# Inner sums of w_out operands made in the last unit of the first product, and turned attention tensors in another layout

## The chip, the cores and the metric

The kernel runs on one core of a Trainium2 chip. The metric is the device time of one execution in microseconds (us); lower is better. TensorE (PE) multiplies matrices, VectorE (DVE), ScalarE (ACT) and GpSimd (POOL) work elementwise, and SyncE (SP) issues the DMAs.

## What is computed

Eight batches of attention with pooled keys and values feed one two-layer product with a "snake" activation. All tensors are fp32.

```python
# q, k, v: (B=8, H=8, S=576, D=64); k and v are averaged over groups of 8 rows: Sp = 72
scores = scale * q @ k_p.T
attn = softmax(scores)                    # 576 x 72 for each head
x = (attn @ v_p) laid out as (4608, 512)
h = x @ w_in                              # (512, 2048)
s = sin(alpha * h)
g = h + s * s / (alpha + 1e-9)
out = g @ w_out                           # (2048, 512)
```

## The kernel before

**Stages.** The 4608 tokens are cut into nine units of 512. The first product (x @ w_in, `hidden`) runs unit by unit, u = 0 to 8, and stores g in DRAM (`g_bridge`). Then the second product (g @ w_out, `outputs`) runs over the same nine units. Both use Strassen's scheme in Winograd's form: seven products of half-size blocks instead of eight. The second product uses it on two levels: each of its seven outer products has seven inner ones, and their right-hand operands are sums of blocks of w_out.

**The first product.** A unit has 28 slots: four groups J of seven products. One slot is four matmuls (line 484), which the trace shows as eight. The order of all engines in this stage is written out by hand. `carry(u)` gives a table of extra work by slot: during unit u the attention of batch u + 1 is computed between the products. Slots 1 to 6 hold the scores, slots 8 to 12 the softmax, slots 12 to 14 `turn` (DVE transposes of 32 x 32 blocks into the tile `tr`, line 276). In slots 14 and 15 `move` issues twelve DMAs that carry `tr` to `aT`, the transposed attention weights (line 285). In slots 21 to 24 `turn_q` transposes the q of batch u + 2 into the same tile `tr` (line 145) and moves it with sixteen DMAs (line 152). In slot 24 `values` multiplies `aT` with the pooled v (line 309). This path with DVE transposes holds for batches 2 to 7, that is for units 1 to 6.

After its product a slot leaves work for the next slot: sums of PSUM banks (lines 463 and 544, DVE), the sine and the squares (ACT). Five PSUM banks go round, and a product that needs a bank again waits until DVE or ACT has emptied it.

**w_out.** `load_w_out` is a generator. Its first step issues the four loads in unit 7. Its next four steps each scale a quarter of w_out (line 408) and make outer sums of it (line 410); its last two make the inner sums of operands 1 and 2 (`inner_w`, line 427). `run` advances it in slots 13 and 20 of unit 7 and slots 6, 13, 17 and 20 of unit 8. The inner sums of the other five operands are made in `outputs`, while its first unit runs (`if u == 0 and n < 5: self.inner_w(...)`).

**The second product.** Only the PE order is written by hand; a planner orders the others, DVE among them. The outer products come as `ORDER = (1, 2, 4, 6, 7, 5, 3)`, and their first steps are woven into the last slots of unit 8. For one outer product p, seven calls of `product` (line 747) accumulate into one bank and one tile `ps_y`, of which there are three. `outer` makes the left-hand sums from the four quarters of g (tiles `r`, `home`, `x`), `inner` the inner ones (tiles `xe`, `home`), `combine` puts the results together (tiles `c`, `o`). All their DVE instructions have line 707, the helper `tt`. The DMA of an output block has line 763.

Of the kernel before, what the change touches and what calls it, by code (L numbers as in the profile page):

```python
# [40 lines left out]
class Kernel:  # L41
# [86 lines left out]
    def turn_q(self, b, part):  # L128


        nc = self.nc
        qm = self.qm[b]
        main, rest = self.q_views(qm)
        if part == 0:
            self.tr = self.new_tr()
        tr = self.tr.rearrange("p (c hp t i) -> p c hp t i", hp=self.NP, t=5, i=32)[:, 0:4]
        if part < 2:
            for e in range(2):
                if part == 0:
                    out = tr[:, 2 * e:2 * e + 2, :, 0:4, :].rearrange("p k hp t i -> p hp t k i")  # L140
                    x = main[:, e::2].rearrange("p hp t (k i) -> p hp t k i", i=32)
                else:
                    out = tr[:64, 2 * e:2 * e + 2, :, 4, :].rearrange("p k hp i -> p hp k i")
                    x = rest[:, e::2].rearrange("p hp (k i) -> p hp k i", i=32)
                nc.vector.transpose(out=out, in_=x)
            return
        self.qt[b] = qt = self.qt_view(qm)
        for a in ((0, 1), (2, 3))[part - 2]:
            w = 160 if a < 2 else 128
            for c in range(4):  # L150
                flat = lambda x: x.rearrange("p hp t i -> p hp (t i)")[:, :, 0:w]
                nc.sync.dma_start(out=flat(qt[32 * c:32 * c + 32, a]), in_=flat(tr[32 * a:32 * a + 32, c]))

    def new_tr(self):
        return self.ap.tile([P, 24 * 5 * 32], F32, name="tr")[:]

    def qt_view(self, t):
        return t[:].rearrange("p (a hp t i) -> p a hp t i", hp=self.NP, a=4, t=5)

    def qt_tiles(self, b):  # L160

        return self.qt[b].rearrange("p a hp t i -> p (a hp t i)").rearrange("p (i hp n) -> p i hp n", i=5, hp=self.NP)

    def attention(self, b):
# [16 lines left out]
        def q_t(i):  # L181

            n = rows[i]
            pairs = self.qm[b][:n, i * H * D:(i + 1) * H * D].rearrange("p (hp d) -> p hp d", hp=NP)
            if b not in self.qt:
                self.qt[b] = self.qt_view(self.qp.tile([P, 5 * H * D], F32, name="q"))
            ps = self.ps_a.tile([P, NP, P], F32, name="ps_qt", tag="a")
            for hp in range(NP):
                nc.tensor.transpose(ps[:, hp, :n], pairs[:, hp], self.ident[:n, :n])  # L189
            nc.scalar.copy(out=self.qt_tiles(b)[:, i, :, :n], in_=ps[:, :, :n])  # L190

        def columns(hp, i):

            if b < 2:
                return [(c, self.qt_tiles(b)[:, i, hp, c:c + 64]) for c in range(0, rows[i], 64)]
            if i < 4:
                return [(64 * c, self.qt[b][:, i, hp, 2 * c:2 * c + 2].rearrange("p t i -> p (t i)")) for c in range(2)]
            return [(32 * a, self.qt[b][:, a, hp, 4]) for a in range(2)]

# [60 lines left out]
        def new_a():  # L260
            aT.append(self.ap.tile([Sp, 4, H, 5, 32], F32, name="aT"))

        def a_t(i, g):
            n = rows[i]
            ps = self.ps_a.tile([Sp, 4, P], F32, name="ps_at", tag="a")
            for hh in range(4):
                nc.tensor.transpose(ps[:, hh, :n], ex[:n, i, 4 * g + hh, 0:Sp], self.ident[:n, :n])  # L267
            cp = nc.scalar.copy if g == 0 else nc.vector.tensor_copy
            cp(out=aT[0][:, 0:n // 32, 4 * g:4 * g + 4, i, :].rearrange("k a h i -> k h a i"),
               in_=ps[:, :, :n].rearrange("k h (a i) -> k h a i", i=32))  # L270

        def turn(i):
            n = rows[i]
            if i == 0:
                self.tr = self.new_tr().rearrange("p (c h t i) -> p c h t i", c=3, h=H, i=32)
            nc.vector.transpose(out=self.tr[:n, :, :, i, :].rearrange("p c h i -> p h c i"),
                                in_=ex[:n, i].rearrange("p h (c i) -> p h c i", i=32))

        def move(part):
            for a in (2 * part, 2 * part + 1):  # L280
                w = 160 if a < 2 else 128
                for c in range(3):
                    m = min(32, Sp - 32 * c)
                    flat = lambda x: x.rearrange("k h t i -> k h (t i)")[:, :, 0:w]
                    nc.sync.dma_start(out=flat(aT[0][32 * c:32 * c + m, a]), in_=flat(self.tr[32 * a:32 * a + m, c]))  # L285

# [16 lines left out]
        def values(hp):  # L303
            vp = self.vp[b]
            ps = self.ps_a.tile([P, 4 * P], F32, name="ps_o", tag="a")
            for e in range(2):
                h = 2 * hp + e
                x = aT[0][:, :, h, 0:4, :].rearrange("k a t i -> k t a i" if b < 2 else "k t a i -> k t (a i)")
                nc.tensor.matmul(ps[64 * e:64 * e + 64, :], vp[:, h, :], x, start=True, stop=True)  # L309
            to_x(ps[:].rearrange("p (t j) -> p j t", t=4), hp, 0, 512)  # L310

        def values_rest():
            vp = self.vp.pop(b)
            ps = self.ps_a.tile([P, NP, 64], F32, name="ps_or", tag="a")
            for hp in range(NP):
                for e in range(2):
                    h = 2 * hp + e
                    nc.tensor.matmul(ps[64 * e:64 * e + 64, hp, :], vp[:, h, :], aT[0][:, 0:2, h, 4, :], start=True, stop=True)
            to_x(ps[:], slice(0, NP), 512, 64)
# [5 lines left out]
    def load_alpha(self, row, rows):  # L325
# [4 lines left out]
        self.rat = self.const.tile([P, self.K2], F32, name="rat")  # L330
        self.alb = self.new_tr()[:, 0:self.FF]
        self.al_row, self.al_rows = row[0:1], rows[:self.K2]
# [17 lines left out]
    def load_w_in(self):  # L350

        nc, h = self.nc, self.FF // 2
        blk = lambda n: self.wp.tile([P, 2, h], F32, name=n)
        a11, a12, a21, a22, s1, s2, s4 = (blk(n) for n in ("a11", "a12", "a21", "a22", "as1", "as2", "as4"))
        self.A = {1: a11, 2: a12, 3: s4, 4: a22, 5: s1, 6: s2, 7: a21}
# [37 lines left out]
    def load_w_out(self, wp):  # L393
# [22 lines left out]
        self.W = {}  # L416
        for p in (1, 2):
            yield
            self.inner_w(p, wp)
        yield  # L420

    def inner_w(self, p, wp):
        nc, NJ = self.nc, self.NJ
        x = self.wb[p]
        e = wp.tile([P, 3, NJ, P], F32, name=f"we{p}")
        b = lambda i, j: x[:, :, i - 1, j - 1, :]
        tt = lambda o, x, y: nc.vector.tensor_tensor(out=o, in0=x, in1=y, op=OP.subtract)
        t1, t2, t4 = (e[:, i] for i in range(3))
        tt(t1, b(1, 2), b(1, 1))
# [182 lines left out]
    def carry(self, u):  # L612
# [43 lines left out]
        elif u < last:  # L656
# [9 lines left out]
            for hp in range(4):  # L666
                at((0, 1, 3, 4)[hp], self.load_kv, "v", b, hp)
                if b < last:
                    at((12, 13, 14, 17)[hp], self.load_kv, "k", b + 1, hp)
                at(24, A.values, hp)  # L670
            at(24, A.values_rest)
            if b < last:
# [29 lines left out]
    def outputs(self):  # L702
# [41 lines left out]
        def product(st, q, out, start):  # L744
            A, W = st["A"][q], self.W[st["p"]][q]
            for J in range(self.NJ):
                nc.tensor.matmul(out, A[:, J, :], W[:, J, :], start=(start and J == 0), stop=(J == self.NJ - 1), skip_group_check=True)  # L747

# [3 lines left out]
        def combine(st):  # L752
# [22 lines left out]
            elif p in (2, 3):  # L775
                o = block("o", 4)
                add(o[:], c[1 if p == 2 else 3][:], x4)
                with_z(o)
                out(0, 0 if p == 2 else 1, o)
# [16 lines left out]
        for k in range(len(seq) + 1):  # L796
# [19 lines left out]
            if last:  # L816
                product(last, 5, last["yz"][:, 1, :], False)
                product(last, 4, last["x"][:, 2, :], False)
            if st:
                product(st, 6, x[:, 1, :], False)  # L820
# [3 lines left out]
                if k + 1 < len(seq) and seq[k + 1] not in A:  # L824
                    A[seq[k + 1]] = inner(seq[k + 1][0], ORDER[seq[k + 1][1]])
                if u == 0 and n < 5:
                    self.inner_w(ORDER[n + 2], self.gs)
# [11 lines left out]
    def run(self):  # L839
        nc, tc = self.nc, self.tc  # L840
        pool = lambda s, n, b, **kw: s.enter_context(tc.tile_pool(name=n, bufs=b, **kw))
        with ExitStack() as top:
# [7 lines left out]
            nc.gpsimd.memset(self.ones[:], 1.0)  # L850
            engines = {nc.tensor.engine, nc.vector.engine, nc.scalar.engine, nc.gpsimd.engine, nc.sync.engine}
            with ExitStack() as one:
                self.wp = pool(one, "wp", 1)
# [23 lines left out]
                for u in range(self.NU):  # L877
                    x = self.carry(u)
                    if u == self.B - 1:
# [5 lines left out]
                        next(w)  # L885
                        for i in (13, 20):
                            x[i].append(lambda: next(w))
                    elif u > self.B - 1:
                        for i in (6, 13, 17, 20):
                            x[i].append(lambda: next(w))  # L890
# [47 lines left out]
```

## Time and profile before

| what | value |
|---|---|
| median of 3 runs | 961.09 us (961.07 to 962.59) |
| profiled execution, own time | 961.07 us |
| its span | 959.3 us |
| PE busy | 937.3 us, 98% of the span |
| DVE busy | 675.1 us, 70% |
| ACT busy | 414.5 us, 43% |
| second product, from its first product to the end | 550.3 to 959.3 us |
| one unit of the first product (units 1 to 5), from one `values` to the next | 57.2 us |

The span runs from the first instruction to the last; 1.8 us of the execution's own time lie outside it. The granted TensorE clock is 1.000 over the whole span. "Busy" counts modelled ends of matmuls, which overlap, so a wait of PE is best read from the starts of two matmuls and from the idle time that the trace puts before one.

### The profile page before, as it was taken

Reading aid. Unit: us, or ns where it says so; the run is one execution under the profiler, and the core shown is the slowest. Engines: PE = TensorE matmul, PEld = TensorE weight load, DVE = VectorE, ACT = ScalarE, POOL = GpSimd, SP = SyncE. Lnnn points to the kernel's source line nnn. Section 1 sums busy time; section 2 is a strip of 40 time slices with the busy share of each in tenths; the row PEclk is TensorE's granted clock in tenths of the full one; section 3 lists DMA queues with packets and bytes.
Section 4 is the critical chain, followed back from the end, with each engine's and each line's share of the span. In section 5 each row is a group of like instructions: output and inputs, shape, how many; then the busy total and the mean of one; then the engine's idle time right before and its main releaser. Section 6 shows DMA issues by size and latency. Waiting matters only on the chain.

```text
span 959.3 us, 18142 instructions
## 1 busy us (share of the span) xinstructions
PE 937.3 (98%) x7259; PEld 833.8 (87%) x7259; DVE 675.1 (70%) x1070; ACT 414.5 (43%) x919; POOL 200.6 (21%) x215
## 2 busy tenths in 40 slices
PE   7999999999999999999999999999999999999998
PEld 4677787887878888787888888999999999999998
DVE  4889584766838576583366889968678685958684
ACT  4377466575756647576565531111111111111111
POOL 1718374443725445260000000000000000000000
PEclk9999999999999999999999999999999999999999
DMA  9537466766576664636615135324242434243200
GB/s 223 170 97 208 128 191 145 212 147 201 162 196 202 149 187 114 187 124 183 224 77 206 80 126 193 120 102 154 79 155 69 151 97 153 98 149 122 100 34 35
DMA packets 84038, 137.88 MB, mean 144 GB/s; under 512 B 10177, under 2 KB 49873, under 8 KB 79345
## 3 DMA queue, kind: packets, MB, share of 16 engines
q1 hardware_dynamic: 83920, 136.70, 46.8%
q8 instruction: 58, 0.95, 0.4%
q14 instruction: 26, 0.21, 0.1%
q10 hardware_dynamic: 34, 0.02, 0.0%
HBM read 74.47 MB, written 47.19 MB: 127 GB/s over the span
## 4 chain that ended last, share of the span: by engine, by line
PE 86%; DVE 6%; DMA 2%; POOL 2%; issue 1%; SPq 1%; ACT 1%; DVEq 0%; POOLq 0%
PE bank L484 39%; PE bank L747 28%; PE ps_y L747 11%; PE ps_o L309 3%; PE ps_sc L208 2%; POOL kvin L105 1%; DMA q<-in_q_dram 1%; SPq L285 1%; DMA kvin<-in_v_dram 1%; DVE sm L257 1%; DVE as L368 1%; DVE h L544 1%; DVE h L463 1%; PE ps_qt L189 1%; PE ps_at L267 1%
## 5 line engine op out<-in xcount | busy, mean ns | idle before, releaser
L484 PE MATMUL bank<-home,a 128*128 128x256 f32 x1152 | 266.3, 382 | 1.4 <-ACT bank L514 1.4
L484 PEld LDWEIGHTS bank<-home,a 128*128 128x128 f32 x1152 | 215.3, 190 | 35.1 <-ACT bank L514 2.1
L484 PE MATMUL bank<-home,as 128*128 128x256 f32 x864 | 201.6, 382 | 3.4 <-DVE as L368 1.6
L484 PEld LDWEIGHTS bank<-home,as 128*128 128x128 f32 x864 | 161.7, 190 | 27.3 <-ACT bank L502 2.9
L105 POOL TENSOR_TENSOR kvin<-kvin 72x512 f32<-72x512 f32 x112 | 130.1, 1162 | 179.1 <-DMA kvin<-in_v_dram 111.1
L463 DVE TENSOR_TENSOR h<-bank,p 128x512 f32<-128x512 f32 x72 | 49.1, 682 | 82.9 <-ACT s L492 54.2
L490 ACT ACTIVATE s<-h,rat 128x256 f32<-128x256 f32 x144 | 65.2, 500 | 88.8 <-DVE h L463 88.8
L747 PE MATMUL bank<-wb,home 128*128 128x128 f32 x712 | 92.1, 275 | 0.0
L747 PEld LDWEIGHTS bank<-wb,home 128*128 128x128 f32 x712 | 85.7, 192 | 0.0
L821 ACT COPY bank<-bank 128x128 f32<-128x128 f32 x63 | 15.8, 250 | 149.7 <-PE bank L747 149.7
L492 ACT ACTIVATE s<-s 128x512 f32<-128x512 f32 (+1 forms) x106 | 77.8, 768 | 1.1
L490 ACT ACTIVATE s<-bank,rat 128x256 f32<-128x256 f32 x144 | 60.1, 468 | 36.3 <-PE bank L484 25.7
L747 PE MATMUL bank<-wb,xe 128*128 128x128 f32 x512 | 67.6, 275 | 0.0
L747 PEld LDWEIGHTS bank<-wb,xe 128*128 128x128 f32 x512 | 62.4, 192 | 0.1
L747 PE MATMUL bank<-we,home 128*128 128x128 f32 x464 | 59.4, 276 | 1.1 <-DVE home L707 1.1
L834 ACT COPY bank<-bank 128x128 f32<-128x128 f32 x63 | 15.8, 250 | 96.6 <-PE bank L747 96.6
L747 PEld LDWEIGHTS bank<-we,home 128*128 128x128 f32 x464 | 55.6, 192 | 1.3 <-issue 1.3
L250 POOL TENSOR_TENSOR ex<-ex,sm 128x576 f32<-128x576 f32 (+1 forms) x38 | 42.5, 1149 | 44.7 <-ACT ex L239 25.5
L544 DVE TENSOR_TENSOR h<-h,s 128x1024 f32<-128x1024 f32 x36 | 44.8, 1244 | 0.0
L544 DVE TENSOR_TENSOR h<-bank,s 128x512 f32<-128x512 f32 x36 | 24.5, 681 | 25.3 <-ACT s L492 24.0
L813 ACT COPY bank<-ps_y 128x256 f32<-128x256 f32 x63 | 22.5, 357 | 39.0 <-PE ps_y L747 39.0
L514 ACT COPY bank<-bank 128x512 f32<-128x512 f32 x36 | 20.6, 572 | 39.4 <-PE bank L484 39.4
(139 smaller groups left out, 1434.2 us busy)
## 6 DMA issues: line engine op xcount, KB each, us to landing
g_bridge<-h SPq DMA_DIRECT2D x36, 1024.0 KB
r<-g_bridge SPq DMA_DIRECT2D x18, 1024.0 KB
home<-g_bridge SPq DMA_DIRECT2D x18, 1024.0 KB
out_dram<-o SPq DMA_DIRECT2D x36, 256.0 KB
q<-in_q_dram SPq DMA_DIRECT2D x8, 1024.0 KB
kvin<-in_k_dram SPq DMA_DIRECT2D x28, 288.0 KB
kvin<-in_v_dram SPq DMA_DIRECT2D x28, 288.0 KB
a<-in_moe_w_in_dram SPq DMA_DIRECT2D x16, 256.0 KB
```

Of the source, the lines that this page charges most:

```text
L105: (eng or nc.gpsimd).tensor_tensor(out=o, in0=t[:, :, 0:w], in1=t[:, :, w:2 * w], op=OP.add)
L208: nc.tensor.matmul(ps[e][r:r + q.shape[-1], hp, :], q[s], kb[s, hp, :], start=True, stop=True)
L250: eng.tensor_tensor(out=E(n, i, 0, H), in0=E(n, i, 0, H), in1=sm[:n].unsqueeze(2).to_broadcast([n, H, Sp]), op=OP.mult)
L309: nc.tensor.matmul(ps[64 * e:64 * e + 64, :], vp[:, h, :], x, start=True, stop=True)
L463: add = lambda o, x, y: nc.vector.tensor_tensor(out=o, in0=x, in1=y, op=OP.add)
L484: nc.tensor.matmul(ps[:, jj, :], self.A[p][:, kk, f * P:(f + 1) * P], x[:, kk, :], start=(start and jj == 0 and kk == 0), stop=(kk == 1), ...
L490: nc.scalar.activation(out=G.s[:, i, j, jj, :], in_=src[:, jj, :], func=AF.Sin, scale=self.rat[:, f:f + 1])
L492: square = lambda G, x: nc.scalar.activation(out=x, in_=x, func=AF.Square)
L514: nc.scalar.copy(out=G.b7[:], in_=G.b6[:])
L544: add = lambda o, x, y: nc.vector.tensor_tensor(out=o, in0=x, in1=y, op=OP.add)
L747: nc.tensor.matmul(out, A[:, J, :], W[:, J, :], start=(start and J == 0), stop=(J == self.NJ - 1), skip_group_check=True)
L813: nc.scalar.copy(out=x[:, 0:2, :], in_=yz[:, 0:1, :].to_broadcast([P, 2, P]))
```

## The change

There are four parts.

1. **Inner sums.** `load_w_out` makes five operands' inner sums, 1, 2, 4, 6 and 7, and does it in slots 10, 13, 14, 17 and 20 of unit 8. The sums of 4, 6, 7 and 5 go into slices of the w_in operands a11, a12 and s4 of which `hidden` has made its last use; these three tiles move to a pool that lasts to the end. Three quarters of w_out are scaled in unit 7 (slots 9, 14, 20), the fourth in slot 6 of unit 8. `outputs` makes the sums of operands 5 and 3 only; on DVE they end up before the outer sums of the second product's first unit.
2. **Layout.** In `tr`, the turned q and `aT` the head becomes the outer index and the row block the inner one. A transpose of q takes one instruction for all heads instead of two. The moves of 160 columns per head, which read and wrote 5120 contiguous bytes per partition for `aT` and 2560 for q, become runs of 640 bytes; the moves of 128 columns stay at 512 bytes.
3. **values.** In units 1 to 6 the four calls of `values` go from slot 24 to slots 23, 24, 24 and 25, and `values_rest` goes to slot 25. A call in a slot's table comes ahead of the slot's product.
4. **The last addition.** For outer product 3 the term z from `ps_y` is added to `c3` before the last sum instead of to the output after it.

```diff
@@ load_w_out
-        for p in (1, 2):
+        for p in (1, 2, 4, 6, 7):
             yield
             self.inner_w(p, wp)
@@ inner_w
-        e = wp.tile([P, 3, NJ, P], F32, name=f"we{p}")
-        t1, t2, t4 = (e[:, i] for i in range(3))
+        if p in (4, 6, 7, 5):
+            J = (4, 6, 7, 5).index(p)
+            t1, t2, t4 = (self.A[i][:, :, J * JW * P:(J + 1) * JW * P].rearrange("p k (j d) -> p k j d", j=2) for i in (1, 2, 3))
+        else:
+            e = wp.tile([P, 3, 2, 2, P], F32, name=f"we{p}")
+            t1, t2, t4 = (e[:, i] for i in range(3))
@@ turn_q
-                nc.vector.transpose(out=out, in_=x)
+            nc.vector.transpose(out=tr[:, 0:16, 0:4, :].rearrange("p (h k) t i -> p h t k i", k=2),
+                                in_=main.rearrange("p h t (k i) -> p h t k i", i=32))
...
-                nc.sync.dma_start(out=flat(qt[32 * c:32 * c + 32, a]), in_=flat(tr[32 * a:32 * a + 32, c]))
+                src = tr[32 * a:32 * a + 32, 0:16].rearrange("p (hp c) t i -> p hp c (t i)", c=4)[:, :, c, 0:w]
+                nc.sync.dma_start(out=qt[32 * c:32 * c + 32, :, a].rearrange("p hp t i -> p hp (t i)")[:, :, 0:w], in_=src)
@@ attention
-            aT.append(self.ap.tile([Sp, 4, H, 5, 32], F32, name="aT"))
+            aT.append(self.ap.tile([Sp, H, 4, 5, 32], F32, name="aT"))
...
-                    nc.sync.dma_start(out=flat(aT[0][32 * c:32 * c + m, a]), in_=flat(self.tr[32 * a:32 * a + m, c]))
+                    src = self.tr[32 * a:32 * a + m].rearrange("p (h c) t i -> p h c (t i)", c=3)[:, :, c, 0:w]
+                    nc.sync.dma_start(out=aT[0][32 * c:32 * c + m, :, a].rearrange("k h t i -> k h (t i)")[:, :, 0:w], in_=src)
@@ carry
-                at(24, A.values, hp)
-            at(24, A.values_rest)
+                at((23, 24, 24, 25)[hp], A.values, hp)
+            at(25, A.values_rest)
@@ combine and the loop of outputs
                 add(o[:], c[1 if p == 2 else 3][:], x4)
-                with_z(o)
+                if p == 2:
+                    with_z(o)
...
+                if last["p"] == 3:
+                    t, z = C[last["u"]][3], last["yz"]
+                    tt(t[:, :, 1, :], t[:, :, 1, :], z[:, 1:2, :].to_broadcast([P, 2, P]), OP.add)
...
-                if u == 0 and n < 5:
+                if u == 0 and n in (3, 4):
                     self.inner_w(ORDER[n + 2], self.gs)
@@ run
-                        for i in (13, 20):
+                        for i in (9, 14, 20):
...
-                        for i in (6, 13, 17, 20):
+                        for i in (6, 10, 13, 14, 17, 20):
```

More of the change, by code (lines that the diff above doesn't have):

```diff
@@ L134, in turn_q @@
         if part == 0:
[L135 to L145, printed above, removed]
+            self.tr = self.ap.tile([P, 24, 5, 32], F32, name="tr")
+        tr = self.tr
+        if part == 0:
+            nc.vector.transpose(out=tr[:, 0:16, 0:4, :].rearrange("p (h k) t i -> p h t k i", k=2),
+                                in_=main.rearrange("p h t (k i) -> p h t k i", i=32))
+            return
+        if part == 1:
+            nc.vector.transpose(out=tr[:64, 0:16, 4, :], in_=rest.rearrange("p h (k i) -> p (h k) i", i=32))
             return
@@ L150, in turn_q @@
             for c in range(4):
-                flat = lambda x: x.rearrange("p hp t i -> p hp (t i)")[:, :, 0:w]
-                nc.sync.dma_start(out=flat(qt[32 * c:32 * c + 32, a]), in_=flat(tr[32 * a:32 * a + 32, c]))
-    def new_tr(self):
-        return self.ap.tile([P, 24 * 5 * 32], F32, name="tr")[:]
+                src = tr[32 * a:32 * a + 32, 0:16].rearrange("p (hp c) t i -> p hp c (t i)", c=4)[:, :, c, 0:w]
+                nc.sync.dma_start(out=qt[32 * c:32 * c + 32, :, a].rearrange("p hp t i -> p hp (t i)")[:, :, 0:w], in_=src)
     def qt_view(self, t):
-        return t[:].rearrange("p (a hp t i) -> p a hp t i", hp=self.NP, a=4, t=5)
-    def qt_tiles(self, b):
-        return self.qt[b].rearrange("p a hp t i -> p (a hp t i)").rearrange("p (i hp n) -> p i hp n", i=5, hp=self.NP)
+        return t[:].rearrange("p (hp a t i) -> p hp a t i", hp=self.NP, a=4, t=5)
     def attention(self, b):
@@ L189, in q_t @@
                 nc.tensor.transpose(ps[:, hp, :n], pairs[:, hp], self.ident[:n, :n])
-            nc.scalar.copy(out=self.qt_tiles(b)[:, i, :, :n], in_=ps[:, :, :n])
+            nc.scalar.copy(out=self.qt[b].rearrange("p hp a t i -> p hp (a t i)")[:, :, P * i:P * i + n], in_=ps[:, :, :n])
         def columns(hp, i):
[L194 to L198, printed above, removed]
+            qt = self.qt[b].rearrange("p hp a t i -> p hp (a t i)")
+            if b < 2 or i < 4:
+                return [(c, qt[:, hp, (P if b < 2 else 160) * i + c:][:, :64]) for c in range(0, rows[i], 64)]
+            return [(32 * a, qt[:, hp, 160 * a + P:160 * a + 160]) for a in range(2)]
         def products(i):
@@ L268, in a_t @@
             cp = nc.scalar.copy if g == 0 else nc.vector.tensor_copy
-            cp(out=aT[0][:, 0:n // 32, 4 * g:4 * g + 4, i, :].rearrange("k a h i -> k h a i"),
-               in_=ps[:, :, :n].rearrange("k h (a i) -> k h a i", i=32))
+            cp(out=aT[0][:, 4 * g:4 * g + 4, 0:n // 32, i, :], in_=ps[:, :, :n].rearrange("k h (a i) -> k h a i", i=32))
         def turn(i):
@@ L274, in turn @@
             if i == 0:
-                self.tr = self.new_tr().rearrange("p (c h t i) -> p c h t i", c=3, h=H, i=32)
-            nc.vector.transpose(out=self.tr[:n, :, :, i, :].rearrange("p c h i -> p h c i"),
-                                in_=ex[:n, i].rearrange("p h (c i) -> p h c i", i=32))
+                self.tr = self.ap.tile([P, 24, 5, 32], F32, name="tr")
+            nc.vector.transpose(out=self.tr[:n, :, i, :], in_=ex[:n, i].rearrange("p h (k i) -> p (h k) i", i=32))
         def move(part):
@@ L283, in move @@
                     m = min(32, Sp - 32 * c)
-                    flat = lambda x: x.rearrange("k h t i -> k h (t i)")[:, :, 0:w]
-                    nc.sync.dma_start(out=flat(aT[0][32 * c:32 * c + m, a]), in_=flat(self.tr[32 * a:32 * a + m, c]))
+                    src = self.tr[32 * a:32 * a + m].rearrange("p (h c) t i -> p h c (t i)", c=3)[:, :, c, 0:w]
+                    nc.sync.dma_start(out=aT[0][32 * c:32 * c + m, :, a].rearrange("k h t i -> k h (t i)")[:, :, 0:w], in_=src)
         def to_x(ps, hp, t0, m):
@@ L307, in values @@
                 h = 2 * hp + e
-                x = aT[0][:, :, h, 0:4, :].rearrange("k a t i -> k t a i" if b < 2 else "k t a i -> k t (a i)")
+                x = aT[0][:, h, :, 0:4, :].rearrange("k a t i -> k t a i" if b < 2 else "k t a i -> k t a i")
                 nc.tensor.matmul(ps[64 * e:64 * e + 64, :], vp[:, h, :], x, start=True, stop=True)
@@ L317, in values_rest @@
                     h = 2 * hp + e
-                    nc.tensor.matmul(ps[64 * e:64 * e + 64, hp, :], vp[:, h, :], aT[0][:, 0:2, h, 4, :], start=True, stop=True)
+                    nc.tensor.matmul(ps[64 * e:64 * e + 64, hp, :], vp[:, h, :], aT[0][:, h, 0:2, 4, :], start=True, stop=True)
             to_x(ps[:], slice(0, NP), 512, 64)
@@ L330, in load_alpha @@
         self.rat = self.const.tile([P, self.K2], F32, name="rat")
-        self.alb = self.new_tr()[:, 0:self.FF]
+        self.alb = self.ap.tile([P, 24, 5, 32], F32, name="tr")[:].rearrange("p k t i -> p (k t i)")[:, 0:self.FF]
         self.al_row, self.al_rows = row[0:1], rows[:self.K2]
@@ L352, in load_w_in @@
         nc, h = self.nc, self.FF // 2
-        blk = lambda n: self.wp.tile([P, 2, h], F32, name=n)
+        blk = lambda n: (self.wq if n in ("a11", "a12", "as4") else self.wp).tile([P, 2, h], F32, name=n)
         a11, a12, a21, a22, s1, s2, s4 = (blk(n) for n in ("a11", "a12", "a21", "a22", "as1", "as2", "as4"))
@@ L422, in inner_w @@
     def inner_w(self, p, wp):
-        nc, NJ = self.nc, self.NJ
+        nc = self.nc
         x = self.wb[p]
-        e = wp.tile([P, 3, NJ, P], F32, name=f"we{p}")
-        b = lambda i, j: x[:, :, i - 1, j - 1, :]
+        b = lambda i, j: x[:, :, i - 1, j - 1, :].rearrange("p (k j) d -> p k j d", k=2)
         tt = lambda o, x, y: nc.vector.tensor_tensor(out=o, in0=x, in1=y, op=OP.subtract)
-        t1, t2, t4 = (e[:, i] for i in range(3))
+        if p in (4, 6, 7, 5):
[4 more added lines that the diff above has]
+            t1, t2, t4 = (e[:, i] for i in range(3))
         tt(t1, b(1, 2), b(1, 1))
@@ L746, in product @@
             for J in range(self.NJ):
-                nc.tensor.matmul(out, A[:, J, :], W[:, J, :], start=(start and J == 0), stop=(J == self.NJ - 1), skip_group_check=True)
+                nc.tensor.matmul(out, A[:, J, :], W[:, J // 2, J % 2, :], start=(start and J == 0), stop=(J == self.NJ - 1), skip_group_check=True)
         def block(n, bufs=1):
@@ L851, in run @@
             engines = {nc.tensor.engine, nc.vector.engine, nc.scalar.engine, nc.gpsimd.engine, nc.sync.engine}
+            self.wq = pool(top, "wq", 1)
             with ExitStack() as one:
```

## The prediction

> **What bounds the kernel now.** I read the busy shares first, then the waits of PE, then the chain that ended last and the timeline where the chain leaves PE.
>
> ```profile
> PE 937.3 (98%) x7259; PEld 833.8 (87%) x7259; DVE 675.1 (70%) x1070; ACT 414.5 (43%) x919; POOL 200.6 (21%) x215
> ```
>
> PE bounds the kernel. A gain must take a wait out of PE, and any new wait of PE adds its whole length. The waits of PE sum to 17 us, and most lie before 100 us, in code that the change hardly touches. Later there is one cluster, in the chain from 560 to 600 us (start, length, what):
>
> ```profile
> 566.03 2.20 DVE x L707
> ...
> 569.17 2.20 DVE x L707
> ...
> 571.43 2.06 issue
> 573.49 1.90 DVE home L707 x3
> 575.39 0.14 issue
> 575.53 3.82 PE bank L747 x32
> 579.35 2.27 issue
> 581.62 2.02 PE ps_y L747 x16
> ```
>
> Here the second product takes over. The "issue" pieces hide a cause, which the timeline of the same stretch names:
>
> ```profile
> 578.90 2.29 DVE L707 TENSOR_TENSOR home<-r,x 128x2048 f32<-128x2048 f32 x1
> ...
> 581.11 0.42 DVE L707 TENSOR_TENSOR o<-o,ps_y 128x256 f32<-128x256 f32 x1
> ...
> 581.62 1.13 PE L747 MATMUL ps_y<-wb,home 128*128 128x128 f32 x8 [2.29 <-issue]
> ```
>
> The product wants one of three `ps_y` tiles. The addition that empties it sits in DVE's queue behind a 2.29 us sum and ends at 581.53; PE starts 0.09 us later. Outer products open at 564.75, 571.52 and 581.62, that is 6.77 and 10.10 us apart, where the later ones stand at 6.25 (589.90 to 596.15 in the chain). So **4.4 us** are lost: 0.5 for `x`, 1.25 for `home` at 575.53, 2.45 for `ps_y`, the rest in restarts. DVE is busy without a gap from 560 to 582 us.
>
> The timeline of unit 2 shows the other place:
>
> ```profile
> 204.54 3.86 SPq L285 DMA_DIRECT2D aT<-tr  x6
> ...
> 209.17 4.44 SPq L285 DMA_DIRECT2D aT<-tr  x6
> ...
> 214.70 3.62 PE L484 MATMUL bank<-home,as 128*128 128x256 f32 x16
> ...
> 217.53 3.02 DVE L145 STREAM_TRANSPOSE tr<-q 128x1024 f32<-128x1024 f32 x4 [4.79 <-DMA aT<-tr]
> 218.25 3.65 PE L309 MATMUL ps_o<-aT,vp 72*64 72x512 f32 x16
> ```
>
> The PE row from 214.70 is slots 22 and 23. DVE waits 4.79 us for the last move of `aT`, since it overwrites `tr`. `values` at 218.25 waits for the same moves and comes just late enough not to stand.
>
> [...] in unit 2 a 5120-byte packet takes 392 ns, and a 512-byte one 38 to 40 where the queue is quiet, about 13 bytes per ns both. [...] No packet of 640 bytes is in this trace.
>
> **The change part by part.**
>
> *Inner sums.* A set is four sums of 0.69 us (line 427), 2.5 us back to back. Four sets (4, 6, 7 and 5) and that of 3 leave the stretch from 561.74 to 591.5 us. Two of these, 8 sums or 5 us, stand within the cluster, 561.74 to 578.31. The planned order of the changed kernel has all sets ahead of the first outer sum. I play DVE forward: set 5's rest and set 3 fill 556.3 to 559.8, where DVE stood until 560.00 for ACT; the two sums for line 544 end at 561.85; `x5` 561.85 to 564.05 (its load landed at 560.1 by the landing records); three `xe` sums to 565.85; `x6` to 568.05; `xe`, `c`, `x7` to 571.2; the three `home` sums to 573.1; two sums and the `ps_y` addition to 574.6. PE without waits needs `x6` at 571.0, `home` at 573.7 and the free `ps_y` at 577.25. All three come in time, the second by 0.6 us. Gain 4.4; I take **4.2**, bounds 1.5 and 4.4.
>
> *What unit 8 pays.* Its DVE loses a quarter of scaling (4.6 us: 2.18 + 2.62 less overlap) and gains three sets and two early sums (9 us). Slots 13 and 14 now hold two sets, 5.1 us, where one quarter took 4.6: what follows is 0.4 later, then the set of 6 ends about 540.5, and the addition due at 540.39 ends near 541.3; its product starts at 541.86. Before slot 27 the addition of 553.37 moves to about 554.65 and ends at 555.35, against a product at 555.73. Both covers hold by 0.4 to 0.6 us; if they fail, PE stands up to 1 us twice. Cost 0, bounds 0 and 2. In unit 7 the first quarter now falls near 475 us; its loads landed at 465.7, and DVE had idle time of 4.5 us before 479.61. Cost 0; if a load came late, the additions queued behind would hold PE.
>
> *The last addition.* At the end `o<-c,bank` starts at 955.08 and the `ps_y` addition ends at 956.22. With the latter made early (DVE idles 2.16 us there), the output is ready at 955.77: gain **0.45**, bounds 0.3 and 0.7.
>
> *values a slot earlier.* Slot 23 starts 8 x 0.216 us into the PE row that begins slot 22. If PE wants `aT` there, it starts when DVE does now, since both wait for the same moves: in unit 4, where both stood, DVE started at 332.67 and PE at 332.74. Start of slot 23 and start of DVE: 159.23 and 160.22; 216.43 and 217.53; 273.64 and 274.53; 330.84 and 332.67; 388.13 and 389.21. The differences 0.99, 1.10, 0.89, 1.83 and 1.08 sum to 5.9. PE gives 0.1 of start-up back and stands 0.1 in unit 4 already: **5.7 us** lost with the moves as they are. In unit 6 no key load cuts in between and they land 0.4 us before slot 23. [...] ACT's copies out of `ps_o` move along and gate nothing.
>
> *Layout.* The first six moves now have 256 runs like the last six, whose issue takes 4.15 to 4.44 us instead of 3.86: +0.3 on SP, in front of a key load and the last six. [...] I take landings **0.3 us later**, bounds 0.7 earlier and 1.0 later; that is 5 x 0.3 and 0.1 in unit 6, 1.6 us. DVE's transposes: two of 1.22 and two of 0.39 become one of each at twice the length, by the line through these durations (118 ns + 1.08 per element) 2.33 + 0.67 against 3.23: 0.2 us less, hidden beside PE. The q moves land by 234.1 in unit 2; their last rows are wanted two slots and more after 235.75. Cost 0; if they slip 2 us, the scores of slots 4 and 5 stand. ACT and DVE copies into the new layout keep their element counts: 0.
>
> *Sum:* -4.2 - 0.45 + 5.7 + 1.6 = **+2.7 us** on the profiled execution's own 961.07 us (span 959.3 and 1.8 around it), which is the median to 0.02: 963.8 us.
>
> **The rivals.** *B, the moves land earlier* and the change gains. The 5120-byte packets took 392 ns each where they filled the engines, 298 at best; short runs may interleave better, and the short q moves land within 2.0 us of issue, the long `aT` ones in 2.4. Against it: the last six moves already are short and set the landing. Each tenth of a us earlier gives back 0.5; from 0.6 earlier the kernel is measurably faster. At 0.7 earlier: 5.7 - 3.5 - 4.65 = -2.4, **958.7 us**. *C, short runs are dear under load.* While loads and stores mix in (212 to 214 us), a 512-byte packet takes 54 ns by the median. At 67 for 640 bytes a move costs 1.07 us of all engines instead of 0.78, some 1.2 for six; landings 1.0 later, 0.8 of it in unit 6: 5.7 + 5.0 + 0.8 - 4.65 = +6.9, **968 us**. *D, the handover keeps its wait*: the work pushed into unit 8 reaches PE, or DVE still comes late, and only 1.5 is gained: 963.8 + 2.7 = **966.5 us**.
>
> **How the numbers follow.** A measurement here can tell some 0.2% (1.9 us) from no change. My forecast has 0.50, own range 961.5 to 966: 0.15 of it within 0.2%, 0.35 slower. B has 0.25: 0.18 faster, 0.07 within. C has 0.15 and D 0.10, slower but for 0.03. So faster 0.18, same 0.25, slower 0.57. The range 958.6 to 968.2 leaves out about half of B and a third of C.
>
> **What would show it.** Right: in the changed profile PE waits for `aT` moves before line 309's product in five units, 1.0 to 2.1 us each; the period of those units is 58.3 us or more instead of 57.2; outer products from 564 us on open 6.25 to 6.5 us apart; the last two DVE additions are one. Wrong: no wait before `values` (B), waits above 2.2 us each (C), or waits on line 707 sums after 560 us that remain (D).

## The result, and the profile after

The kernel after took **975.46 us** (median of four: 973.10, 974.41, 976.52, 979.29), the kernel before 961.60 on the same chip (961.07 to 962.59): ratio 1.0147, 95% interval 1.0111 to 1.0183. That is 13.9 us slower, where 2.7 were forecast. The profiled execution is the slowest of the four: own time 979.29 us, span 977.5, that is 18.2 us more than the 961.07 and 959.3 of before. The four stand in the order of their mean granted TensorE clocks: 1.000 at 973.10 us, 0.996 at 974.41, 0.995 at 976.52 and 0.991 at 979.29. The fastest, with no clock lost in that mean, is still 11.5 us over the median of before, so most of the median's loss has other causes.

A line number is that of the run's own kernel. In the kernel after, 476 is the large product of the units (484 before), 296 `values` (309), 272 `move` (285), 138 `turn_q` (145) and 739 `product` of the second product (747); line 100 loads keys and values. PEld is PE's loading of weights, SPq SyncE's issuing of a DMA.

The busy shares of the kernel after come first.

```profile
PE 950.6 (97%) x7259; PEld 835.9 (86%) x7259; DVE 676.9 (69%) x1058; ACT 413.7 (42%) x919; POOL 202.4 (21%) x215
```

PE issues as many instructions as before, 7259, but is busy 13.3 us longer. So part of the loss isn't waiting: the same matmuls took longer. That was in no step of the prediction.

The handover to the second product, in the chain that ended last (start, length, what):

```profile
572.02 0.89 PE ps_y L739 x8
...
579.88 1.79 PE ps_y L739 x16
581.66 4.62 PE bank L739 x40
586.28 1.79 PE ps_y L739 x16
588.07 4.47 PE bank L739 x40
592.53 1.79 PE ps_y L739 x16
594.32 4.47 PE bank L739 x40
```

Every piece of the stretch is PE; the DVE sums and "issue" pieces of before are gone. Outer products open at 579.88, 586.28 and 592.53, 6.40 and 6.25 us apart, where before it was 6.77 and 10.10. From 572 to 599 us PE's starts gain 4.4 us on the same starts of before: what was lost there is back.

The waits of PE between 110 and 560 us (what waited, what for, us in total, times, longest):

```profile
PE ps_o L296 <- DMA aT<-tr: 7.1, 4, 2.1
PE ps_o L296 <- POOL kp L105: 1.6, 1, 1.6
PE ps_sc L197 <- issue: 0.4, 1, 0.4
```

Measured from one PE start to the next, `values(0)` start 1.69, 1.87, 1.76, 1.97, 2.25 and 0.38 us later than usual in units 1 to 6. The change of product costs 0.11 us of that even without a wait (in before, beyond the 0.216 us of the record ahead of it, 0.09 in five units and 0.18 in unit 4, 0.11 by the mean); the rest is PE standing, 1.58, 1.76, 1.65, 1.86, 2.14 and 0.27, in sum 9.3 us. Waits below are meant in this way. The second line is the wait of unit 3, and the POOL that it names had ended at 282.25 us; DVE, which waits for the moves, starts at 282.42 and PE at 282.44, so it is the moves there too. The timeline of unit 2 shows DVE and PE waiting for them until the same instant.

```profile
207.47 4.65 SPq L272 DMA_DIRECT2D aT<-tr  x6
212.22 0.99 SPq L100 DMA_DIRECT2D kvin<-in_k_dram  x1
213.27 4.36 SPq L272 DMA_DIRECT2D aT<-tr  x6
217.63 1.89 PE L476 MATMUL bank<-home,as 128*128 128x256 f32 x8
221.22 2.31 DVE L138 STREAM_TRANSPOSE tr<-q 128x2048 f32<-128x2048 f32 x1 [5.55 <-DMA aT<-tr]
221.23 1.08 PE L296 MATMUL ps_o<-aT,vp 72*64 72x512 f32 x4 [1.71 <-DMA aT<-tr]
222.24 3.21 PE L476 MATMUL bank<-home,as 128*128 128x256 f32 x8
225.38 2.36 PE L296 MATMUL ps_o<-aT,vp 72*64 72x512 f32 x8
```

Compare the PE rows at 217.63 and 222.24: the same eight records of the large product, 1.89 us before the wait and 3.21 after it. What lies between is seen in a table of stretches for the kernel after: the stretch, its length, PE busy in it with its instructions, the granted clock as a share of full speed, the share of the DMA engines and GB/s.

```profile
158.01:161.42 3.41, 1.88 (x10) 1.00 1.10 284
161.42:164.83 3.41, 3.41 (x14) 1.00 0.57 197
219.45:222.86 3.41, 1.70 (x8) 1.00 0.93 318
222.86:226.27 3.41, 3.41 (x9) 0.50 0.31 90
403.77:407.18 3.41, 1.32 (x6) 1.00 0.98 326
407.18:410.59 3.41, 3.41 (x10) 0.50 0.25 87
```

From 222.86 us on **TensorE is granted half its clock for 3.41 us**. The clock record has five such stretches ahead of the end: at 96.57, 222.86, 284.30, 345.74 and 407.18 us, each 3.413 us long, each starting a whole number of 3.413 us after the others. The first has a counterpart between 96.7 and 98.3 us in six of the runs below (e1, e2, e8 to e11); the other four follow the waits of units 2 to 5. Unit 1 waited 1.58 us and kept its clock. From one start to the next, a record of the large product takes 0.216 us ahead of the wait (217.63 to 219.14) and 0.427 in this stretch (223.11 to 224.82). So I estimate that 3.41 us at half clock do the work of 1.71: four stretches cost 6.8 us, all five 8.5, which is most of PE's 13.3.

### The profile page after: what moved, and what is told of

Same layout as the page of the kernel before. It is cut to its first block, busy times and chain, and to the rows that moved or that the text cites. A ratio compares the mean times of both kernels' runs of the same rounds, so it can differ in the third digit from the quotient of the medians.

```text
span 977.5 us, 18140 instructions
## 1 busy us (share of the span) xinstructions
PE 950.6 (97%) x7259; PEld 835.9 (86%) x7259; DVE 676.9 (69%) x1058; ACT 413.7 (42%) x919; POOL 202.4 (21%) x215
## 4 chain that ended last, share of the span: by engine, by line
PE 77%; DVE 10%; SPq 4%; DMA 4%; ACT 3%; issue 2%; POOL 0%; DVEq 0%; ACTq 0%
PE bank L739 29%; PE bank L476 28%; PE ps_y L739 12%; SPq L272 4%; PE ps_o L296 3%; PE ps_sc L197 2%; DVE tr L264 2%; DVE sm L246 2%; DMA aT<-tr 2%; DMA kvin<-in_k_dram 1%; DMA q<-in_q_dram 1%; DVE h L455 1%; DVE a L359 1%; DVE as L355 1%; ACT s L482 1%
## 5 line engine op out<-in xcount | busy, mean ns | idle before, releaser
L476 PE MATMUL bank<-home,as 128*128 128x256 f32 x864 | 209.2, 391 | 3.3 <-DVE as L355 1.6
L476 PEld LDWEIGHTS bank<-home,as 128*128 128x128 f32 x864 | 164.9, 194 | 33.3 <-issue 6.3
L296 PE MATMUL ps_o<-aT,vp 72*64 72x512 f32 x128 | 33.9, 637 | 9.2 <-DMA aT<-tr 7.1
L699 DVE TENSOR_TENSOR xe<-home 128x512 f32<-128x512 f32 x30 | 19.4, 687 | 25.5 <-PE bank L739 25.4
```

The lines of the kernel that those rows point to most:

```text
L476: nc.tensor.matmul(ps[:, jj, :], self.A[p][:, kk, f * P:(f + 1) * P], x[:, kk, :], start=(start and jj == 0 and kk == 0), stop=(kk == 1), ...
```

## The experiments

Each kernel ran on one chip beside the kernel before; ratios are against that. Theory T after the result: the layout delays the landings by over 1 us, the earlier `values` wait for them, long waits bring half clock, and the rest of the change gains as predicted. The rivals: unit 8 takes part of the gain back; the layout costs by itself; the order of `values` brings the half clock.

### e1_sums_only

The early inner sums and the early last addition; the old layout, `values` in slot 24.

> The kernel before with two of the four parts: the inner sums made early and the last addition made early; layout and slots of values as before. Theory T (the handover and the end gained as predicted, and all of the loss lies in units 1 to 6): 961.1 - 4.2 - 0.45 = 956.4 us, outer products from 564 us on 6.25 to 6.5 us apart, no stretch of half clock before the end. Rival H (part of the loss is what unit 8 pays for the added sums, and the handover keeps a wait): 959 us or more, with a wait of PE over 1 us between 505 and 585 us.

Measured: 959.11 us, ratio 0.9970 (0.9960 to 0.9981). A gain, but of 2.3 us, not 4.65. Rival H has the time, 959 us or more, but not the cause: from 505 to 585 us PE has no new wait of over 0.25 us, and its starts gain 4.4 us at the handover. What the expectation missed stands after 600 us, once in each outer unit (in e1 and e8, line 712 is `tt` and 752 `product`):

```profile
604.34 1.29 DVE L712 TENSOR_TENSOR xe<-r 128x512 f32<-128x512 f32 x2
605.23 0.97 PEld L752 LDWEIGHTS bank<-we,r 128*128 128x128 f32 x8
605.54 0.69 DVE L712 TENSOR_TENSOR xe<-xe,r 128x512 f32<-128x512 f32 x1
606.35 0.74 PEld L752 LDWEIGHTS bank<-we,xe 128*128 128x128 f32 x6
```

Eight weight loads follow each other 0.11 us apart, so after 605.23 the next should come at 606.12; it comes at 606.35. The `xe` sum, 605.54 to 606.23, is late, and in front of the `xe` sums DVE now does the early addition (604.01, 0.42 us). PE loses 0.22 us in each of eight outer units.

### e8_inner_sums_only and e9_end_addition_once

e8 leaves the early addition out. e9 makes it early only where no further product follows (against e1):

```diff
-                if p == 2:
+                if p == 2 or k < len(seq):
                     with_z(o)
...
-                if last["p"] == 3:
+                if last["p"] == 3 and not st:
```

> The kernel before with the early inner sums alone, without the early last addition. In the trace of both parts together PE waits about 0.2 us once in every outer unit behind the xe sum in front of which the early addition stands. Theory E (the early addition costs 0.2 us in each of eight or nine outer units and gains 0.45 at the end): this kernel is 1.8 - 0.45 = 1.3 us faster than e1_sums_only, 957.8 us at the same clocks, and the waits of 0.15 us after 600 us are gone. Rival F (these small waits come from the early inner sums, whose operands now lie in w_in's parts): the waits stay and this kernel is 0.45 us slower than e1_sums_only, 959.6 us.

> The kernel of e1_sums_only, but with the early addition of the last product only where no further product follows, so once, at the very end. Theory E (the early addition gains 0.45 us there and costs 0.2 us in every earlier outer unit): the waits of 0.15 us after 600 us are gone and the end is 0.45 us shorter, 957.7 - 0.45 = 957.2 us. Rival: the end gains nothing, 957.7 us.

Measured: e8 957.67 us, ratio 0.9944 (0.9928 to 0.9960); e9 956.62 us, ratio 0.9946 (0.9931 to 0.9961). In both the small waits after 600 us are gone, as theory E has it; e8's trace of the same place:

```profile
604.63 1.28 DVE L712 TENSOR_TENSOR xe<-r 128x512 f32<-128x512 f32 x2
605.84 0.68 DVE L712 TENSOR_TENSOR xe<-xe,r 128x512 f32<-128x512 f32 x1
605.85 0.97 PEld L752 LDWEIGHTS bank<-we,r 128*128 128x128 f32 x8
606.74 0.64 PEld L752 LDWEIGHTS bank<-we,xe 128*128 128x128 f32 x5
```

The loads of `xe` follow at once, 0.89 us after the eight before them. From PE's last start to the end of the span it is 4.58 us before, 4.58 in e8 and 4.12 in e9: the addition gains 0.46 at the end. Made early in all outer units it costs 8 x 0.22 = 1.76 and gains 0.46, net 1.3 us lost. e9, which beats both kernels, is about 5 us faster than before; its times can't tell it from e8.

### e2_layout_only and e4_values_back

e2 is the kernel before with the new layout. e4 is the kernel after with

```diff
-                at((23, 24, 24, 25)[hp], A.values, hp)
-            at(25, A.values_rest)
+                at(24, A.values, hp)
+            at(24, A.values_rest)
```

> The kernel before with the new layout alone; values stay in slot 24. Theory T (the new layout makes the aT moves land 1.1 us later): slot 24 had 0.74, 0.63, 0.84, -0.10 and 0.65 us in hand (1.73 less the differences of the prediction), so PE waits 0.4, 0.5, 0.3, 1.2 and 0.5 us in front of values, 2.8 in all, with no stretch of half clock, since none of the waits is near 1.8 us: 963.8 us. Rival L (the layout is no part of it; the moves land late only because values came earlier): 961.1 us, landings as before. Rival X (the layout costs elsewhere too): over 966 us.

> The kernel after with values put back in slot 24: layout, inner sums and last addition as in the kernel after. Theory T: the waits shrink to the 2.8 us of the layout alone and every stretch of half clock goes: 961.1 + 2.8 - 4.65 = 959.2 us, slightly faster than the kernel before. Rival L: 956.4 us. Rival X (the layout brings the loss, wherever values stand): 968 us or more.

Measured: e2 962.01 us, ratio 0.9998 (0.9988 to 1.0007); e4 958.20 us, ratio 0.9959 (0.9943 to 0.9975). Theory T's 1.1 us was too much. DVE's transpose of q starts when the last move of `aT` has landed; counted from the unit's first turn that is 18.50, 18.61, 18.40, 19.34 and 18.59 us in units 1 to 5 of before, 18.82, 19.05, 19.06, 19.10 and 19.36 in e2: 0.39 later by the mean, and `values` in slot 24 wanted them at 19.33. e4 waits a total of 0.5 us in two units. So the layout costs nothing measurable by itself, and only the earlier `values` make it count. And no unit from 1 to 6 has half clock in either profile.

### e3_values_early_only and e6_early_unsplit

The kernel before with `values` as early as in the kernel after, in e3 split over three slots as there, in e6 in one piece:

```diff
# e3
+                at((23, 24, 24, 25)[hp], A.values, hp)
+            at(25, A.values_rest)
# e6
+                at(23, A.values, hp)
+            at(23, A.values_rest)
```

> The kernel before with values in slots 23, 24, 24, 25 alone; layout as before. Theory T (the wait is as long as the landings make it, and the half clock follows waits of about 1.8 us and more): waits of 1.0, 1.1, 0.9, 1.8 and 1.1 us, 5.7 in all, and at most one stretch of half clock (after the 1.8 us): 966.8 us, or 968.5 with it. Rival S (the order of values between the product's slots brings the half clock, however long the wait): five stretches of half clock in front of slot 24, 1.7 us each: 975 us. Rival N (the waits don't come with the moves as they were): 961.1 us.

> The kernel before with all of values and its rest in slot 23: early, but not split. Theory P: the waits of e3_values_early_only stay (5.4 us in five units), the 3.6 us of the split go: 961.4 + 5.4 = 966.8 us, up to 968.5 with one stretch of half clock. Rival Q: 972 us as with the split, or only the half clock less.

Measured: e3 972.14 us, ratio 1.0105 (1.0087 to 1.0124). Neither T's 966.8 to 968.5 nor S's 975. Its profile has waits of 0.94, 0.64, 0.87, 1.49 and 1.04 us, 5.0 in all, near the 5.7 expected, and one stretch of half clock in the units, at 337.66 us after the longest wait (one more, at 593.66, follows the handover's 2.45 us wait). With the waits and one or two stretches of 1.7 us taken from the 10.7 us lost, 2 to 4 us were without a cause: the period that ends with the 0.64 us wait is 58.55 us, which is 57.20 and 0.64 and 0.7 that is no wait. That gave theory P, the price of the split.

e6: 969.67 us, ratio 1.0074 (1.0060 to 1.0089); its profiled execution 966.75. Two of its periods are 58.30 and 58.26 us, and the waits that end them 1.08 and 1.04: with the old 57.20 next to nothing is left over, so P. The two others, 58.21 and 58.82, end with waits of 0.52 and 0.98 and hold 0.47 and 0.63 us more; these stand at 240 and 356 us, where a product of the scores starts late, and not at `values`. The timed runs lie above P's range; their mean clocks, 0.996 in five of six, are those of two stretches of half clock, where I had allowed for one.

### e5_split_no_wait

```diff
-                at(24, A.values, hp)
-            at(24, A.values_rest)
+                at((24, 25, 25, 26)[hp], A.values, hp)
+            at(26, A.values_rest)
```

> The kernel before with the four products of values in slots 24, 25, 25, 26 and the rest in 26: as split up as in the kernel after, but a slot later than it, so that no move of aT is late. Theory P (each change of PE from the large product to values and back costs about 0.3 us, and the split has two more such changes in each of six units): 6 x 0.6 = 3.6 us more, 961.4 + 3.6 = 965.0 us, the period of the units 57.8 instead of 57.2 us, no stretch of half clock. Rival Q (the split itself costs nothing, what was lost beyond the waits is all half clock): 961.4 us, period 57.2.

Measured: 965.79 us, ratio 1.0033 (1.0020 to 1.0046), periods of 57.84 to 58.40 us where before has 57.20 to 57.29, and a clock of 1.000 in the profile. The two shortest, 57.84 and 57.85, are the split alone, 0.65 us for two more interruptions; the longer ones hold late scores as well. Theory P, and the timeline of PE in unit 3 shows where it goes:

```profile
277.70 1.08 PE L309 MATMUL ps_o<-aT,vp 72*64 72x512 f32 x4
278.71 1.99 PE L484 MATMUL bank<-home,a 128*128 128x256 f32 x8
280.64 1.94 PE L309 MATMUL ps_o<-aT,vp 72*64 72x512 f32 x8
282.50 1.99 PE L484 MATMUL bank<-home,a 128*128 128x256 f32 x8
284.43 1.08 PE L309 MATMUL ps_o<-aT,vp 72*64 72x512 f32 x4
285.34 0.64 PE L318 MATMUL ps_or<-aT,vp 72*64 72x64 f32 x16
```

Take the starts. Eight records of the large product fill 280.64 - 278.71 = 1.93 us between two pieces of `values`, and 8 x 0.216 = 1.73 where it runs on: 0.2 more. Four records of `values` fill 278.71 - 277.70 = 1.01, where the sixteen in one piece of before take 3.49, that is 0.87 for four: 0.14 more. One more interruption costs **0.33 us** (half of the 0.65), and the split makes two in each of six units: 3.9 us. No wait shows it; PE counts as busy.

### e7_filled_wait

```diff
+    def fill(self, u):
+        ps = self.ps_a.tile([P, 512], F32, name="ps_f", tag="a")
+        for _ in range(3):
+            self.nc.tensor.matmul(ps[:, 0:256], self.ident[:], self.xT[u][:, 0, 0:256], start=True, stop=True)
...
+                if hp == 0 and b < last:
+                    at(23, self.fill, u)
                 at((23, 24, 24, 25)[hp], A.values, hp)
```

> The kernel after with three products of the identity with xT, 1.3 us in all and read by nobody, in front of values(0) in units 1 to 5: PE works through most of its wait for the moves, and values start when they did. Theory C (the half clock answers PE's standing still): no stretch of half clock from 110 to 560 us, where the profiled run of the kernel after had four; with about three such stretches of 1.7 us in its median, 975.5 - 5.1 + 5 x 0.25 for the added change of weights = 971.6 us. Rival D (the half clock comes from the split order or from the layout's transfers): the stretches stay, 975 us or more.

Measured: 972.25 us, ratio 1.0103 (1.0089 to 1.0116). No stretch of half clock is in its profile ahead of the end, and three of five runs have a mean clock of 1.000. Two pairs of stretches around the start of `values` (units 2 and 4; columns as above):

```profile
217.10:220.51 3.41, 3.27 (x16) 1.00 1.09 281
220.51:223.92 3.41, 3.39 (x14) 1.00 0.56 202
336.90:340.30 3.40, 2.74 (x13) 1.00 1.06 309
340.30:343.70 3.40, 3.40 (x14) 1.00 0.43 147
```

Layout, moves and split are those of the kernel after. Only PE's standing still was filled. With more work the kernel was faster by the medians, 972.25 against 975.46 us, but the two ratios' intervals still touch (1.0116 and 1.0111), so the times alone don't show it. The clocks are the firmer evidence: three of four executions of the kernel after have means of 0.991 to 0.996, none of e7's five is under 0.998. That is theory C's: with the standing filled, the profile has no half clock in the units. (The 0.25 us for a change of weights in the expectation was an estimate.)

### e10_after_old_layout

The kernel after without the layout's edits.

> The kernel after with the old layout of tr, qt and aT; inner sums, last addition and slots of values as in the kernel after. Theory A (the parts add up; late values make the layout's later landings count): e3_values_early_only 972.1 - 4.4 for the inner sums + 1.3 for the early addition = 969.0 us, waits in front of values(0) of 5 us in all instead of 9.3, at most one stretch of half clock between 110 and 560 us. Rival B (the layout is free, as it was alone with values in slot 24): 975 us, like the kernel after.

Measured: 968.05 us, ratio 1.0067 (1.0051 to 1.0083). Theory A; the waits in front of `values` are 0.85, 0.61, 0.49, 1.17 and 0.82 us, 3.9 in all, and no unit from 1 to 6 has half clock. Beside the kernel after the layout is worth 7 us here and nothing in e2. The 9.3 - 3.9 = 5.4 us of longer waits explain most of it; the rest agrees in size with the half clock (mean clocks of 0.996 to 0.999 here, 0.991 to 1.000 in the kernel after).

### e11_key_load_later

```diff
-                    at((12, 13, 14, 17)[hp], self.load_kv, "k", b + 1, hp)
+                    at((12, 13, 16, 17)[hp], self.load_kv, "k", b + 1, hp)
```

> The kernel after with the third key load of a unit issued in slot 16 instead of 14, so that on SP it no longer stands between the first six and the last six moves. Theory S (SP's issue sets the landings; in unit 2 the seventh move is issued 2.4 us after the sixth): the last six are issued about 1.2 us earlier, land 0.7 to 1.2 us earlier, the waits shrink from 9.3 us to 3.3 to 5.8, and the stretches of half clock go: 966 to 969 us. Rival T (the DMA engines' transfers set them): the waits stay at 1.7 to 2.2 us each, 975 us.

Measured: 963.18 us, ratio 1.0014 (1.0006 to 1.0022), 12 us less than the kernel after by one number in the code. Unit 2 of its timeline:

```profile
205.84 9.49 SPq L272 DMA_DIRECT2D aT<-tr  x12
215.44 0.59 SPq L100 DMA_DIRECT2D kvin<-in_k_dram  x1
217.83 2.31 DVE L138 STREAM_TRANSPOSE tr<-q 128x2048 f32<-128x2048 f32 x1 [3.79 <-DMA aT<-tr]
217.85 1.08 PE L296 MATMUL ps_o<-aT,vp 72*64 72x512 f32 x4
```

The first turn stands at 200.22, so the moves have landed 17.61 us after it, 19.37 in the kernel after. Over units 1 to 5 they land 1.86 us earlier by the mean, and PE waits at most 0.15 us. Rival T is wrong; theory S has the direction, but the landings moved more than its 0.7 to 1.2 us, and the time is 3 us below its range. Of it SP explains less than it claimed: the last move is issued 8.75 us after the first instead of 9.45, 0.7 earlier. The rest lies between issue and landing. The key load is no longer issued ahead of the last six; what its own transfer did to them was not separated. What remains against before agrees with the other runs: 962.4 + 3.9 split + 1.3 addition - 4.4 handover = 963.2.

## Why the prediction was wrong

The profiled execution lost 18.2 us, and the starts of `values` tell where. From unit 1 to unit 6 they lie 304.67 us apart instead of 286.10: **+18.6**. From there to the end it is 0.7 less, and ahead of unit 1's 0.4 more. The 18.6 are 7.7 of waits in five units, 3.3 of split, 6.8 of half clock, and 0.8 left over, of which a late start of the scores, 0.7 us at 368 us, is most; its cause is open (the q moves of which the prediction warned had landed by 360.2 us). The 0.7 less is the handover's 4.4 and the end's 0.5, against 1.8 of early additions, unit 6's split, and `values(0)` standing a slot earlier.

1. *Handover, predicted -4.2.* Right. After 560 us nothing is left of the 4.4; "Cost 0" for unit 8 held too (e1, e8).
2. *The last addition, predicted -0.45.* Wrong, +1.3. The gain at the end is there (0.46), but the step costed one place of nine. In the other eight the addition moves in front of `xe` sums which DVE finishes just in time. It named no cover there; the code shows that the edit runs in every outer unit.
3. *values a slot earlier, predicted +5.7 with the moves as they are.* The wait was nearly right: 5.0 us in e3. But the step saw only the slot of the first piece. **Splitting was costed at nothing**, without a reason, and costs 3.9 us (e5). The trace of before showed the price: unit 0 splits `values` once, and the period that holds it is 57.56 us against 57.20 of the others, 0.36.
4. *Layout, landings 0.3 later, 1.6 us.* The term was too small: 0.67 us by the mean in the kernel after (19.18, 19.37, 19.25, 19.30 and 19.69 after the first turn), 0.39 in e2. It lies within the bound of 1.0. With 3, waits of 9.3 us stand against 7.3. Of its grounds the trace of before shows SP's alone, 3.86 us of issue against 4.15 to 4.44; what the shorter runs cost the DMA engines was the author's estimate. Measured: among the moves of `aT` in unit 2 of the kernel after a run of 640 bytes takes 53 ns by the median, eight 424, against 392 for one of 5120 bytes in before, 8% more. (B's "298 at best" was misread: of the 864 packets of 5120 bytes 77 took under 290 ns, the shortest 195; no sum hangs on it.) The step put +0.3 us on SP; the sixth move is issued 3.4 us after the first instead of 3.2, as said, but the seventh comes 2.4 us after the sixth instead of 1.4, with the key load in between. e11 shows that this load was the place to look at.
5. *The clock had no step.* PE bounds the kernel and "any new wait of PE adds its whole length", says the prediction at its start, and so each us of wait was priced at one us; its lines held no stretch of half clock ahead of the end. **The waits cost more than their length**, 6.8 us in the profiled execution. Half clock followed the waits of 1.65 to 2.14 us in units 2 to 5, and one of 1.49 in e3, but not that of 1.58 in unit 1. The wait's length alone does not sort them.

The work counted ahead of a stretch, taken apart by products, does so in these profiles. In the kernel after all six stretches, the one at the very end (977.21 us) included, start whole numbers of 3.413 us apart. I took it that such a grid runs on between the stretches in every profile, which was not shown, and counted PE's busy time in every window of it from 15 us on. Over all 13 profiles, nine windows without products of `values` were followed by half clock; they hold at most 1.45 us of work (e8, from 94.84 us), and no such window with 1.50 us or more was (e7, from 95.41 us). Where the 72x64 products of `values` stand in the window, half clock followed 1.32, 1.70, 1.86 and 1.89 us of work in the kernel after and 1.97 in e3, but nothing from 2.29 on (e10, from 336.76 us). Whether the smaller products count for less was not shown; no run was made for it. In unit 1 the window from 158.01 us, which holds the wait of 1.58, has 1.88 us of the large product alone, and no half clock followed. At the handover half clock followed the wait in e3 and e6 (1.44 and 1.12 us of work in the window) and not in before (1.87).

With the right terms the sum is -4.4 + 1.3 + 9.3 + 3.9 = +10.1. The two runs around the median had mean clocks of 0.996 and 0.995, which is 4.4 us of clock lost in 975: +14.5, where the medians show 13.9. The fastest, at a clock of 1.000, lost 11.5, so 1.4 us have no term. Of the rivals, C had the direction of the landings, not their size (1.0 us later; it was 0.67); B and D did not occur.

The prediction's signs of being right all came, or nearly: five waits of 1.58 to 2.14 us against 1.0 to 2.1, periods over 58.3 us, outer products 6.40 and 6.25 us apart, one addition at the end. They tested the waits and the handover, which it had, and could not see the split, the eight early additions and the clock, which it did not.

## What to carry to other kernels

When PE is the bound, a product moved into gaps is priced by its interruptions too: read from the trace what eight matmuls take between two others and what they take in a row. A wait of PE can be paid twice, once standing and once at half clock, as those of 1.65 to 2.14 us were in the kernel after; from its 3.413 us at half clock I estimate that such a wait, grown from 1 to 2 us, costs 2.7 more (1 and 1.7). Whether it does differs between executions, as the mean clocks from 0.991 to 1.000 of the kernel after show. Look for it in the granted clock, since PE's busy time hides it: at half clock PE was busy for all of the 3.41 us. And an edit in a loop is costed in every pass, not at the place for which it was meant.

## What was not expected of the hardware

- In units 2 to 5 of the kernel after waits of PE of 1.65 to 2.14 us were followed by 3.413 us at half clock, 0.9 to 1.9 us after PE had started again (222.86 - 221.23 = 1.63 in unit 2); with 1.3 us of products read by nobody in the wait, the profile has none (e7).
- Counted on a grid taken to run on between the stretches, windows of 3.413 us without 72x64 products and with up to 1.45 us of work were followed by half clock and those with 1.50 or more were not (all 13 profiles); with such products, half clock followed up to 1.97 us (e3).
- An interruption of the 128x128 product by the 72x64 one costs PE 0.33 us in busy time (e5).
- One key load issued behind the moves instead of among them made them land 1.86 us earlier (e11), more than the 0.7 us by which the last was issued earlier.
